# A retention layer and its feed-forward network on one core: the second batch also in halves of 64 tokens, and keys and values loaded head by head for a whole batch

## The chip, the core and the metric

The kernel runs on one core of one Trainium2 chip. The metric is the device time of one execution in microseconds (us), the median over runs. The core has a matrix engine (PE, with its weight loads PEld), a vector engine (DVE), a scalar engine (ACT), GpSimd (POOL), and a sync engine (SP) which here does nothing but issue DMAs, in the order in which the program names them. All DMAs of this kernel are issued by SP.

## The reference

Inputs are `q`, `k`, `v` of shape 4 batches x 8 heads x 768 tokens x 64, and the weights `w_in` (512 x 2048) and `w_out` (2048 x 512). All are float32.

```python
gamma = 1.0 - 2.0 ** (-5.0 - np.arange(H, dtype=np.float32))
for t in range(S):
    state = gamma[None, :, None, None] * state + np.einsum('bhd,bhe->bhde', k[:, :, t], v[:, :, t])
    y[:, :, t] = scale * np.einsum('bhd,bhde->bhe', q[:, :, t], state)
...
h = np.maximum(x @ w_in, 0.0)
return (h * h @ w_out).astype(np.float32)
```

`x` is `y` with the heads side by side: 3072 tokens x 512.

## The kernel before, in words

**Chunks.** Each batch is cut into 6 chunks of 128 tokens, 24 chunks in all, numbered `m` = 0 to 23. The recurrence becomes matrix products within a chunk (scores of `q` against `k`, masked, times `v`) plus the product of `q` with the state that the chunks before have left. Powers of gamma are multiplied into `q` and `k` beforehand by DVE. A matrix product needs `q` and `k` with the head dimension on the partitions, so both are transposed.

**Three ways to attend.** Chunks 0 to 3 go in pairs before the main loop (the `_pair` functions). Chunks 4 to 11 (`attend`, line 941) keep the 128 tokens of a chunk whole: two heads share the partitions in a block diagonal of keys (`k_bd`), the scores are two groups of 4 products of 128 columns, the state is 4, the outputs are 12 (8 in the first chunk of a batch, which has no state yet). In chunks 4 to 7 PE transposes `q` and `k` (`transpose_q` line 362, `transpose_k` line 376) and ACT copies the result; in chunks 8 to 11 a DMA transposes (`dma_transpose_q` line 390, `dma_transpose_k` line 398) and DVE spreads `k` over the diagonal (`spread_k` line 404). Chunks 12 to 23 (`attend2`, line 953) cut a chunk into two halves of 64 tokens and put a pair of heads on the 128 partitions: the scaled keys lie in block-diagonal tiles `ks_bd2s` (`scale_k2` line 638), the values are cast by POOL in three operations (`cast_v2` line 653), the keys are transposed by one DMA of the whole block diagonal (`transpose_k2` line 662, tile `kT`), the scores are one group of 8 products of 64 columns (`scores2` line 671), the state is 4 products for each half (`state2` line 698), the outputs are 16 of 64 columns (`outputs2` line 720).

**Feed-forward network.** It works on blocks: one of 4 chunks, then ten of 2. `ffn_pieces` (line 806) yields after every piece: 4 to 16 products with `w_in` (line 777) with a ReLU on ACT (line 786) and a square on DVE (line 757), or 4 products with `w_out` (line 835). Block 0 has 28 pieces in the loop, every later block 16: eight of the first product, eight of the second.

**The order of work** is written out by hand. `put(place, ...)` (line 930) hangs a step on a place; `before(n)` (line 1000) issues the steps of place `n` after piece `n` and ahead of piece `n+1`. Pieces 5 to 32 are block 0, 33 to 48 block 1, 49 to 64 block 2, 65 to 80 block 3, 81 to 96 block 4, and so on. Every engine, and SP's queue of DMAs, runs its own instructions strictly in this order.

**Transfers.** A load of `q` (`load_q`, line 89) brings 2 chunks, 512 KB. Chunks 4 to 11 load `k` and `v` by chunk, one DMA of 256 KB each (`load_kv`, line 107). Chunks 12 to 23 load them by groups of 3 chunks, 16 DMAs of 96 KB a group, one for a head (`group_loads`, line 121), in tiles `kg` and `vg` of their own. The eight quarters of the weights pass as float32 through a pool of 5 buffers of 1 MB (`wstage`, lines 141 to 153) and are cast to bf16 by DVE, ACT and POOL; a quarter's load waits until the buffer's earlier quarter has been cast. `pack_constants` (line 237) computes the tables that `attend2` needs, at place 50.

Of the kernel before, what the change touches and what calls it, by code (L numbers as in the profile page):

```python
# [9 lines left out]
FP32 = mybir.dt.float32  # L10
BF16 = mybir.dt.bfloat16
# [3 lines left out]
ALU = mybir.AluOpType  # L15
# [4 lines left out]
LDBUFS = 4  # L20

# [3 lines left out]
DMA_FROM = 8  # L25


PACK_FROM = 12

GROUP = 3  # L30
# [3 lines left out]
def kernel(  # L34
# [9 lines left out]
    nc = tc.nc  # L44
    P = nc.NUM_PARTITIONS

    B, H, S, D = q.shape
    DM, DFF = moe_w_in.shape
    C = 128
    NCH = S // C  # L50
    NPAIR = H // 2
    NFB = DFF // 128
    NCB = DM // 128
    NQ = 4
    FPQ = NFB // NQ
    FQ = DFF // NQ
    chunks = [(b, i) for b in range(B) for i in range(NCH)]
    NCHUNK = len(chunks)
# [3 lines left out]
    scale = 1.0 / float(np.sqrt(D))  # L62
# [4 lines left out]
    ldpool = ctx.enter_context(tc.tile_pool(name="ldpool", bufs=LDBUFS // 2))  # L67
    grpool = ctx.enter_context(tc.tile_pool(name="grpool", bufs=2))
    qspool = ctx.enter_context(tc.tile_pool(name="qspool", bufs=2))
    kspool = ctx.enter_context(tc.tile_pool(name="kspool", bufs=4))  # L70
# [6 lines left out]
    wstage = ctx.enter_context(tc.tile_pool(name="wstage", bufs=5))  # L77
# [9 lines left out]
    raw_q, raw_k, raw_v = {}, {}, {}  # L87
# [33 lines left out]
    def group_loads(m):  # L121

        b, i = chunks[m]
        for name, src, to in (("kg", k, raw_k), ("vg", v, raw_v)):
            t = grpool.tile([P, 2 * GROUP, NPAIR, D], FP32, name=name)
            for h in range(H):
                p, hh = divmod(h, 2)
                rows = slice(64 * hh, 64 * (hh + 1))
                nc.sync.dma_start(
                    t[rows, :, p, :],  # L130
                    src[b, h, i * C : (i + GROUP) * C, :].rearrange("(w s) d -> s w d", s=64),
                )
                yield
            for j in range(GROUP):
                to[m + j] = t[:, 2 * j : 2 * j + 2].rearrange("s u p d -> s (u p) d")

    w_in_v = moe_w_in.rearrange("(cb p) f -> p cb f", p=P)
# [3 lines left out]
    def load_w_in(g, parts=1):  # L141
        t = wstage.tile([P, NCB, FQ], FP32, name="w_stage")
        n = FQ // parts
        for j in range(parts):
            nc.sync.dma_start(
                t[:, :, j * n : (j + 1) * n], w_in_v[:, :, g * FQ + j * n : g * FQ + (j + 1) * n]
            )
        staged["in", g] = t

    def load_w_out(g):  # L150
        t = wstage.tile([P, FPQ, DM], FP32, name="w_stage")
        nc.sync.dma_start(t[:], w_out_v[:, g * FPQ : (g + 1) * FPQ, :])
        staged["out", g] = t
# [16 lines left out]
    halves = [slice(0, 64), slice(64, 128)]  # L170
# [160 lines left out]
    def scale_q(m):  # L331
        b, i = chunks[m]
        qs = qspool.tile([P, 2, H, D], BF16, name="qs")
        nc.vector.tensor_tensor(  # L334
            out=qs[:],
            in0=raw_q.pop(m).rearrange("s h r d -> s r h d"),
            in1=qf[:, i : i + 2, :, None].to_broadcast([P, 2, H, D]),
            op=ALU.mult,
        )
        at[m]["qs"] = qs  # L340

    def scale_kv(m):
        b, i = chunks[m]
        ks = kspool.tile([P, H, D], BF16, name="ks")
        nc.vector.tensor_tensor(
            out=ks[:],
            in0=raw_k.pop(m)[:],
            in1=kf[:, i, :, None].to_broadcast([P, H, D]),
            op=ALU.mult,
        )  # L350
        v_bd = v_bds[m % 2]
        vn = raw_v.pop(m)
        nc.gpsimd.tensor_copy(  # L353
            v_bd[:, :, ::3, :], vn.rearrange("s (p hh) d -> s p hh d", hh=2)
        )
        at[m].update(ks=ks, v_bd=v_bd)
# [40 lines left out]

    def dma_transpose_k(m):
        a = at[m]
        kT = kTpool.tile([P, 2 * NPAIR, C], BF16, name="kT")  # L400
        nc.sync.dma_start_transpose(kT[:, 0:NPAIR], a["ks"].rearrange("s h d -> s (h d)"))
        a["kT"] = kT

    def spread_k(m):
        a = at[m]
        kT = a.pop("kT")
        k_bd = k_bds[m % 2]
        for hh in range(2):
            rows = slice(64 * hh, 64 * (hh + 1))
            nc.vector.tensor_copy(k_bd[rows, :, hh, :], kT[rows, 0:NPAIR])  # L410
        a["k_bd"] = k_bd
# [91 lines left out]
    def scale_pair_q(m, r, engine=nc.vector):  # L503
        b, i = chunks[m]
        if r == 0:
            at[m]["qs"] = qspool.tile([P, 2, H, D], BF16, name="qs")
        engine.tensor_tensor(
            out=at[m]["qs"][:, r],
            in0=raw_q[m].rearrange("s h r d -> s r h d")[:, r],
            in1=qf[:, i + r, :, None].to_broadcast([P, H, D]),  # L510
            op=ALU.mult,
        )

    def scale_pair_k(m, r):
        b, i = chunks[m]
        at[m]["ks"] = pair_view(ks_bd2s[m // 2])
        nc.vector.tensor_tensor(
            out=at[m]["ks"][:, r],
            in0=raw_k[m][:, r],
            in1=kfp[:, i + r, :, None].to_broadcast([P, H, D]),  # L520
            op=ALU.mult,
        )
# [115 lines left out]
    def scale_k2(m):  # L638
        b, i = chunks[m]
        ks = ks_bd2s[m % 2]  # L640
        kn = raw_k.pop(m)
        for hh, rows in enumerate(halves):
            nc.vector.tensor_tensor(  # L643
                out=ks[rows, :, hh, :],
                in0=kn[rows],
                in1=kf2[rows, i].rearrange("s u p -> s (u p)")[:, :, None].to_broadcast(
                    [64, 2 * NPAIR, D]
                ),
                op=ALU.mult,
            )  # L650
        at[m]["ks"] = ks

    def cast_v2(m):
        vn = raw_v.pop(m)
        v2 = v2pool.tile([P, 2 * NPAIR, D], BF16, name="v2")
        nc.gpsimd.tensor_copy(v2[:], vn[:])  # L656
        v_bd = v_bd2s[m % 2]
        for hh, rows in enumerate(halves):
            nc.gpsimd.tensor_copy(v_bd[rows, :, hh, :], vn[rows])  # L659
        at[m].update(v2=v2, v_bd=v_bd)  # L660
# [210 lines left out]
    scale_pair_q(0, 0)  # L871
    scale_pair_q(0, 1)
# [8 lines left out]
    scale_pair_q(2, 0, nc.gpsimd)  # L881
    scale_pair_q(2, 1, nc.gpsimd)
# [47 lines left out]
    def put(place, what, *args):  # L930
        parts.setdefault(place, []).append((what, args))

    def attend_q(m, scaled, transposed):
        if m % 2 == 0:
            put(scaled, scale_q, m)
            put(transposed, dma_transpose_q if m >= DMA_FROM else transpose_q, m)

# [3 lines left out]
    def attend(m, scaled, places):  # L941
        by_dma = m >= DMA_FROM
        attend_q(m, scaled, scaled if by_dma else places[0])
        put(places[0], scale_kv, m)
        if by_dma:
            put(places[0], dma_transpose_k, m)
        put(places[1], spread_k if by_dma else transpose_k, m)
        put(places[2], scores, m, 0)
        put(places[3], scores, m, 1)
        put(places[3], state, m)  # L950
        put(places[4], outputs, m)

    def attend2(m, d):
        attend_q(m, d - 17, d - 15)
        put(d - 15, scale_k2, m)
        put(d - 15, cast_v2, m)
        put(d - 13, transpose_k2, m)
        put(d - 6, state2, m, 0)
        put(d - 5, scores2, m)
        put(d - 3, state2, m, 1)  # L960
        put(d, outputs2, m)
# [3 lines left out]
    for m, place in ((5, 10), (6, 14), (7, 18)):  # L965
        put(place, load, m)
# [7 lines left out]
    attend(6, 30, (33, 35, 37, 39, 42))  # L974
    attend(7, None, (40, 42, 44, 46, 49))
    put(50, pack_constants)
    for j, t in enumerate([s_bds[2]] + ks_bd2s + v_bd2s):
        for hh in range(2):
            put(51 + 3 * j + hh, zero_off_diagonal, t, hh)


    done = [55, 62, 70] + [78 + 8 * j for j in range(13)]
    for m, place in ((8, 29), (9, 31), (10, 36)):
        put(place, load, m)
    for m, d in zip(range(8, NCHUNK), done):
        if m < PACK_FROM:
            attend(m, d - 15 if d < 70 else d - 16, (d - 13, d - 7, d - 5, d - 3, d))
        else:
            attend2(m, d)
        if m + 3 < PACK_FROM:  # L990
            put(d - 13, load, m + 3)
        elif m + 3 < NCHUNK and (m + 3) % 2 == 0:
            put(d - 13, load_q, m + 3)
    for m, place in zip(range(PACK_FROM, NCHUNK, GROUP), (43, 67, 92, 116)):
        loads = group_loads(m)
        for j in range(2 * H):
            put(place + 3 * j // 2, next, loads)
        put(place + 3 * H, next, loads, None)
# [43 lines left out]
```

## Time and profile before

| what | us |
|---|---|
| median of 3 runs | 215.21 (214.72 to 242.04) |
| the profiled execution's own time | 214.73 |
| its span | 212.9 |
| PE busy in the span | 204.5 |
| ACT busy | 116.2 |
| DVE busy | 129.4 |
| POOL busy | 50.6 |

The 1.8 us between span and time lie before the first and after the last instruction. The profile gives, for each engine, when an instruction started, how long it ran, and what ended the idle time ahead of it. For SP it gives when a DMA was issued, how long the issue took, and when the data had landed. A "granted clock" of 1.00 means that PE ran at full speed, 0.50 at half. A row with "x4" holds four equal instructions. PE's matrix products overlap in time, so the cost of a group is read from the start of one group to the start of the next, which is what the chain of waits prints.

### The profile page before, as it was taken

To read this page: it belongs to the slowest core of one execution; us is meant where nothing else is said; L and a number is where in the kernel's file an instruction comes from. 1 tells how busy PE (TensorE), PEld (TensorE's weight loads), DVE (VectorE), ACT (ScalarE), POOL (GpSimd) and SP (SyncE) were. 2 spreads that over 40 slices of the span, in tenths; PEclk is the share of its full clock that TensorE was granted. 3 is DMA by queue.
4 is the path that set the end of the run, shared out by engine and by line. 5 is a ranking of instruction groups with operands and counts; after the bars stand their busy time and mean duration, and the time that the engine had idled before them with its cause. 6 is when DMAs were issued, how large, how long until landed. Compare 5 with 4: busy or idle time off the path is not lost.

```text
span 212.9 us, 5128 instructions
## 1 busy us (share of the span) xinstructions
PE 204.5 (96%) x2077; PEld 142.1 (67%) x2077; DVE 129.4 (61%) x257; ACT 116.2 (55%) x216; POOL 50.6 (24%) x106
## 2 busy tenths in 40 slices
PE   5789999999999999999999999999999999999994
PEld 1467644558966975875875875875965965965853
DVE  4777875265585696796495595593694693640410
ACT  8365885358853643652663663652753754643631
POOL 5332466221110411025121323008122223000000
PEclk9889999999999999999999999999999999999999
DMA  6999999999969898599698698998795452401102
GB/s 162 290 317 383 386 386 258 293 242 274 276 172 201 199 197 145 161 207 182 164 197 191 154 189 188 152 194 202 164 240 127 99 80 72 102 0 49 52 0 99
DMA packets 90551, 39.65 MB, mean 186 GB/s; under 512 B 66336, under 2 KB 84000, under 8 KB 90528
## 3 DMA queue, kind: packets, MB, share of 16 engines
q1 hardware_dynamic: 90528, 39.33, 79.4%
q8 instruction: 16, 0.26, 0.6%
q14 instruction: 7, 0.06, 0.1%
HBM read 27.26 MB, written 6.29 MB: 158 GB/s over the span
## 4 chain that ended last, share of the span: by engine, by line
PE 90%; ACT 2%; DVE 2%; DMA 2%; POOL 1%; issue 1%; POOLq 0%; ACTq 0%; DVEq 0%
PE psf L835 38%; PE psf L777 38%; DMA qn<-in_q_dram 2%; PE st L421 2%; PE y L484 1%; PE st L681 1%; PE y L737 1%; PE y L730 1%; PE c_ps L708 1%; PE y L313 1%; DVE pt L568 1%; PE c_ps L585 1%; PE psf L544 1%; ACT osb L845 1%; PE c_ps L447 1%
## 5 line engine op out<-in xcount | busy, mean ns | idle before, releaser
L777 PE MATMUL psf<-xt,w_in_bf 128*128 128x256 bf16 (+2 forms) x880 | 90.7, 259 | 0.2 <-ACT xt L492 0.2
L835 PE MATMUL psf<-w_out_bf,h 128*128 128x512 bf16 (+2 forms) x400 | 89.6, 371 | 0.0
L777 PEld LDWEIGHTS <-w_in_bf 128*128 128x128 bf16 x880 | 71.3, 98 | 11.8 <-issue 0.3
L786 ACT ACTIVATE h<-psf 128x512 bf16<-128x512 f32 x96 | 57.0, 597 | 22.2 <-PE psf L777 19.6
L835 PEld LDWEIGHTS <-h 128*128 128x128 bf16 x400 | 36.3, 98 | 35.1
L757 DVE TENSOR_TENSOR h<-h 128x512 bf16<-128x512 bf16 x96 | 43.1, 467 | 21.0 <-ACT h L786 20.2
L845 ACT ACTIVATE osb<-psf 128x512 f32<-128x512 f32 (+2 forms) x25 | 14.5, 580 | 28.6 <-PE psf L835 28.6
L718 DVE CAST s_bd<-c_ps 64x256 bf16<-64x256 f32 x22 | 9.4, 427 | 27.4 <-ACT s_bd L717 27.1
L656 POOL CAST v<-vg 128x512 bf16<-128x512 f32 x12 | 8.1, 674 | 56.3 <-PE c_ps L708 21.0
L659 POOL CAST v_bd<-vg 64x512 bf16<-64x512 f32 x24 | 16.4, 682 | 15.0 <-PE y L737 14.1
L428 DVE TENSOR_TENSOR pt<-st,cmask 128x512 bf16<-128x512 f32 x16 | 11.1, 692 | 12.5 <-PE st L421 12.3
L643 DVE TENSOR_TENSOR ks_bdp<-kg,kf 64x512 bf16<-64x512 f32 x24 | 18.3, 762 | 0.4
L353 POOL CAST v_bd<-vn 128x512 bf16<-128x512 f32 x8 | 5.7, 718 | 36.2 <-PE y L484 29.1
L744 ACT ACTIVATE xt<-y 128x512 bf16<-128x512 f32 x12 | 8.9, 742 | 9.6 <-PE y L737 9.6
L334 DVE TENSOR_TENSOR qs<-qn,qf 128x1024 bf16<-128x1024 f32 x10 | 12.1, 1213 | 2.1 <-DMA qn<-in_q_dram 2.0
L717 ACT ACTIVATE s_bd<-c_ps 64x256 bf16<-64x256 f32 x22 | 8.1, 367 | 8.8 <-PE c_ps L708 8.8
L301 POOL CAST w_out_bf<-w_stage 128x512 bf16<-128x512 f32 x12 | 7.8, 689 | 5.5 <-DMA w_stage<-in_moe_w_out_dram 5.5
L492 ACT ACTIVATE xt<-y 128x512 bf16<-128x512 f32 x8 | 6.0, 749 | 5.5 <-PE y L484 5.2
L688 DVE TENSOR_TENSOR pt<-st,cmask 128x512 bf16<-128x512 f32 x12 | 8.3, 691 | 0.4
L313 PE MATMUL y<-ident 128*128 128x512 bf16 (+1 forms) x13 | 5.8, 558 | 2.1 <-POOL ident L199 2.1
L708 PEld LDWEIGHTS <-ks_bdp 128*128 128x128 bf16 x88 | 5.6, 98 | 2.6
L737 PE MATMUL y<-pt,v_bd 128*128 128x64 bf16 x96 | 7.0, 193 | 0.0
(99 smaller groups left out, 167.1 us busy)
## 6 DMA issues: line engine op xcount, KB each, us to landing
qn<-in_q_dram SPq DMA_DIRECT2D x12, 512.0 KB, 4.9
out_dram<-osb SPq DMA_DIRECT2D x23, 256.0 KB, 2.5
w_stage<-in_moe_w_out_dram SPq DMA_DIRECT2D x4, 1024.0 KB, 12.2
w_stage<-in_moe_w_in_dram SPq DMA_DIRECT2D x3, 1024.0 KB, 11.8
kg<-in_k_dram SPq DMA_DIRECT2D x32, 96.0 KB, 3.6
vg<-in_v_dram SPq DMA_DIRECT2D x32, 96.0 KB, 3.4
kn<-in_k_dram SPq DMA_DIRECT2D x8, 256.0 KB, 5.6
vn<-in_v_dram SPq DMA_DIRECT2D x8, 256.0 KB, 5.6
```

Source lines behind the costliest of these rows:

```text
L334: nc.vector.tensor_tensor(out=qs[:], in0=raw_q.pop(m).rearrange("s h r d -> s r h d"), in1=qf[:, i : i + 2, :, None].to_broadcast([P, 2, H ...
L428: nc.vector.tensor_tensor(out=a["pt"][:, 2 * half : 2 * half + 2], in0=st[:], in1=cmask.rearrange("s r t -> s (r t)")[:, None, None, :].to ...
L643: nc.vector.tensor_tensor(out=ks[rows, :, hh, :], in0=kn[rows], in1=kf2[rows, i].rearrange("s u p -> s (u p)")[:, :, None].to_broadcast([6 ...
L659: nc.gpsimd.tensor_copy(v_bd[rows, :, hh, :], vn[rows])
L718: nc.vector.tensor_copy(s_bd[halves[1], :, 1, :], c[halves[1]])
L737: nc.tensor.matmul(yv, lhsT=a["v_bd"][:, u * NPAIR + p], rhs=a["pt"][:, u * NPAIR + p, :].rearrange("s (r t) -> s r t", r=2), start=not inter,
L744: nc.scalar.activation(xts[tb][:, :, off : off + C].rearrange("e p (s r) -> e p r s", r=2), y[:], AF.Copy,)
L757: nc.vector.tensor_mul(hv, hv, hv)
L777: nc.tensor.matmul(hp, lhsT=w_in_bf[g][:, cb, fq * 128 : (fq + 1) * 128], rhs=xts[tb][:, cb, cols], start=(cb == 0), stop=(cb == NCB - 1),)
L786: nc.scalar.activation(hv, hp[:], AF.Relu)
L835: nc.tensor.matmul(op[:], lhsT=h_of(tb, f)[:, 0, j * C : (j + 1) * C], rhs=w_out_bf[g][:, fq, cols], start=(f == 0), stop=(f == NFB - 1),)
L845: nc.scalar.activation(osb[:, cols], op[:], AF.Copy)
```

## The change

- Chunks 6 to 11 go the way of `attend2` as well (`PACK_FROM` is 6 instead of 12). `dma_transpose_k` and `spread_k` are gone; the DMA transposes of `q` begin with chunk 6 instead of 8, those of `k` too, and those of `k` in chunks 8 to 11 are of the full block diagonal.
- `k` and `v` of a batch are loaded by `batch_loads`: 8 DMAs for `k`, 8 for `v`, one for a head, 192 KB each. For the second batch they are split in two sets: first the part of chunks 6 and 7 (16 DMAs of 64 KB), later that of chunks 8 to 11 (16 of 128 KB).
- These tiles come from the pool of the weights' quarters, now called `stage`, which has 4 buffers instead of 5. The pools of the groups are gone.
- `q` is scaled in two instructions of half the size, at two places.
- `pack_constants` moves from place 50 to place 14, the clearing of the diagonals from places 51 to 64 to places 15 to 24.
- The outputs of chunks 6 to 11 move: places 42, 49, 55, 62, 70, 78 become 47, 52, 57, 62, 70, 78.

```diff
-PACK_FROM = 12
-GROUP = 3
+PACK_FROM = 6
...
-    wstage = ctx.enter_context(tc.tile_pool(name="wstage", bufs=5))
+    stage = ctx.enter_context(tc.tile_pool(name="stage", bufs=4))
...
+    def batch_loads(m, name, ends):
+        b, i = chunks[m]
+        src, to = (k, raw_k) if name == "k" else (v, raw_v)
+        t = stage_tile(2 * NCH * NPAIR * D)
+        t = t.rearrange("s (p w d) -> s p w d", p=NPAIR, d=D)
+        for j in range(NCH):
+            to[m + j] = t[:, :, 2 * j : 2 * j + 2].rearrange("s p u d -> s u p d")
+        for w0, w1 in zip([0] + ends, ends):
+            for hh, rows in enumerate(halves):
+                for p in range(NPAIR):
+                    nc.sync.dma_start(
+                        t[rows, p, 2 * w0 : 2 * w1],
+                        src[b, 2 * p + hh, w0 * C : w1 * C].rearrange("(w s) d -> s w d", s=64),
+                    )
+                    yield
...
-    def attend2(m, d):
-        attend_q(m, d - 17, d - 15)
-        put(d - 15, scale_k2, m)
-        put(d - 15, cast_v2, m)
-        put(d - 13, transpose_k2, m)
-        put(d - 6, state2, m, 0)
+    def attend2(m, d, before, q_at, k_at, turn_at, v_at):
+        if m % 2 == 0:
+            put(q_at, scale_q, m, 0)
+            put(q_at + 1, scale_q, m, 1)
+            put(q_at + 2, dma_transpose_q, m)
+        put(k_at, scale_k2, m)
+        put(v_at, cast_v2, m)
+        put(turn_at, transpose_k2, m)
+        put(max(d - 6, before), state2, m, 0)
         put(d - 5, scores2, m)
         put(d - 3, state2, m, 1)
         put(d, outputs2, m)
...
-    attend(6, 30, (33, 35, 37, 39, 42))
-    attend(7, None, (40, 42, 44, 46, 49))
-    put(50, pack_constants)
+    put(14, pack_constants)
...
+    put(12, load_q, 6)
+    put(30, load_q, 8)
+    put(41, load_q, 10)
+    done = [47, 52, 57, 62] + [70 + 8 * j for j in range(14)]
+    ahead = {6: (34, 35, 39), 7: (37, 38, 44), 8: (47, 48, 48), 9: (52, 53, 53), 10: (57, 59, 58)}
+    for m, d in zip(range(PACK_FROM, NCHUNK), done):
+        attend2(m, d, done[m - PACK_FROM - 1] if m > PACK_FROM else 0,
+                d - 17 if m < 8 else d - 18, *ahead.get(m, (d - 15, d - 13, d - 15)))
+        if m >= 12 and m % 2 == 0:
+            put(d - 29, load_q, m)
+    places = {
+        (6, "k"): [13 + j // 3 for j in range(8)] + [39 + j // 2 for j in range(8)],
+        (6, "v"): [16 + j // 3 for j in range(8)] + [43 + j // 2 for j in range(8)],
+        (12, "k"): [52 + j for j in range(8)],
+        (12, "v"): [60 + j for j in range(8)],
+        (18, "k"): [84 + 2 * j for j in range(8)],
+        (18, "v"): [100 + 2 * j for j in range(8)],
+    }
```

The numbers that `ahead` gives for a chunk are the places of the scaling of its keys, of the DMA that transposes them, and of the cast of its values. In SP's queue the change leaves, between the load of `q` of chunk 6 and the transpose of chunk 8's keys, this order: 16 loads of 64 KB, 2 stores, `q` of chunk 8, 2 stores, the transposes of `q` 6, `k` 6 and `k` 7, 4 loads of 128 KB, `q` of chunk 10, the transpose of `q` 8, 6 loads of 128 KB, a store, 6 loads of 128 KB, a store.

## The prediction

> **What bounds the kernel now.** I read the page first, then the stretches between the blocks, the chain of waits in order of time, and SP's queue. The page says that PE is the bound:
>
> ```profile
> PE 204.5 (96%) x2077; PEld 142.1 (67%) x2077; DVE 129.4 (61%) x257; ACT 116.2 (55%) x216; POOL 50.6 (24%) x106
> ```
>
> The stretches (columns: length, then busy time and count of PE, PEld, DVE, ACT, POOL, granted clock, DMA share, GB/s) show where it can be shortened:
>
> ```profile
> 5.20:8.60 3.40, 1.85 (x18) 1.01 (x18) 2.46 (x4) 1.77 (x4) 0.00 (x0) 1.00 1.22 290
> 8.70:12.00 3.30, 3.30 (x42) 2.00 (x43) 2.93 (x6) 1.15 (x2) 2.04 (x2) 0.50 1.22 290
> ...
> 67.70:85.56 17.86, 17.59 (x223) 13.62 (x220) 12.83 (x33) 9.02 (x16) 3.91 (x16) 1.00 0.92 191
> 85.56:102.04 16.48, 16.48 (x147) 11.95 (x145) 12.18 (x21) 7.80 (x14) 4.27 (x6) 1.00 0.98 177
> 102.04:117.69 15.65, 15.65 (x159) 11.15 (x157) 10.76 (x19) 8.51 (x17) 3.20 (x6) 1.00 0.94 184
> ```
>
> From 102.04 on chunks 12 to 23 are attended in halves and PE has no gap; nothing there can change but by a wait. The DMA engines are almost always busy up to there (share 0.92 to 0.98), so transfers have little room. The first two rows come back below.
>
> The chain gives PE's price of each step, from the start of one group to the next:
>
> ```profile
> 39.45 0.45 PE tp L367 x8
> 41.62 0.22 PE tp L380 x4
> 43.57 0.22 PE st L421 x4
> 45.74 0.22 PE c_ps L447 x4
> 61.13 0.45 PE y L484 x8
> 67.70 0.89 PE psf L777 x16
> 72.43 0.38 PE st L421 x4
> 102.92 0.23 PE st L681 x8
> ```
>
> Twelve products of outputs cost 0.67 (53.21 to 53.88 in the timeline of PE), sixteen narrow ones 0.47 (123.11 to 123.58), twelve narrow ones 0.35 in proportion, the narrow state 0.11 (120.38 to 120.49).
>
> SP's queue (start, length, issue):
>
> ```profile
> 41.42 0.96 SPq L113 DMA_DIRECT2D kn<-in_k_dram  x1
> 42.42 1.16 SPq L113 DMA_DIRECT2D vn<-in_v_dram  x1
> ...
> 60.56 0.37 SPq L113 DMA_DIRECT2D kn<-in_k_dram  x1
> ...
> 68.54 1.96 SPq L129 DMA_DIRECT2D kg<-in_k_dram  x3
> 70.60 0.56 SPq L847 DMA_DIRECT2D out_dram<-osb  x1
> 71.26 2.48 SPq L401 DMA_TRANSPOSE kT<-ks  x1
> 73.79 0.57 SPq L94 DMA_DIRECT2D qn<-in_q_dram  x1
> ```
>
> An issue costs SP about the same whatever it moves: 0.65 for 96 KB of one head, 0.57 for 512 KB. And the queue already runs behind: the transpose at 71.26 had its keys scaled at 68.3.
>
> **PE's work.** Whole chunks cost: chunk 6 half of 0.45, 0.22, 2 x 0.22, 0.22, 0.45 = 1.56; chunk 7 the same with 0.67 for outputs = 1.78; 8 to 10 without PE's transposes 1.33 each; 11, which gives no state on, 1.11. Together 8.44. In halves: chunk 6 0.23 + 2 x 0.11 + 0.35 = 0.80; 7 to 10 0.92 each; 11 0.81; together 5.29. Saved on the path: **3.15**. The wait at 72.43 (0.27) also goes: DVE was late there because it waited for POOL's tables, which now come at place 14. **-0.27.**
>
> **Tables and clearing at places 14 to 24.** They cost POOL about 2 us between the casts of two quarters of `w_out`; the second then ends near 35.8 instead of 33.8, and its first use is the fifth piece of the second product, near 36.9. ReLUs wait for the exponential about 1 us, and four buffers of PE's results cover that. 0; at most 1.
>
> **Four weight buffers.** The first quarter of `w_out` is issued at 19.2 (when a buffer is cast) instead of 14.29. In the queue of transfers it lands behind the last of `w_in` (26.45) at 29.15 either way, and is needed cast at 33.4. 0; at most 3.5, if the 4.9 of delay came through but for the slack of 1.4.
>
> **DVE, ACT, POOL.** Scaling keys in halves (2 x 0.69 for 0.68), casting values (3 x 0.61 for 0.69), splitting `q` (2 x 0.70 for 1.22) lie beside PE: DVE is busy 12.8 of 17.9 us, POOL 3.9. 0. The later loads (places 52 to 114) are fewer than the groups' and as large. 0.
>
> **SP's queue between places 13 and 48.** Here I expect the loss. From 41.42 (start of chunk 6's `k`, which the same transfers precede as before): 16 loads at 0.65 = 10.4, 4 stores at 0.61, `q` of chunk 8 at 0.63 gives 54.9. The transposes follow: `q` 6 at 1.6, to 56.5, and `k` 6 at 1.35, issued at 56.5. Landings:
>
> ```profile
> L665 SPq DMA_TRANSPOSE kT<-ks_bdp x12: 1239/1292/2412, 95.2 to 181.5; - x12
> ...
> DMA to landing us min/median/max: 3.1/3.4/4.6
> ```
>
> So `k` 6 lands at 59.9. PE wants it at place 42, which was at 61.13 and comes 1.33 - 0.11 earlier, 59.9. **0**, bounds 0 and 1.2. Then `k` 7 to 59.2, and, ahead of `k` 8, 16 loads (10.4), `q` 10 (0.63), the transpose of `q` 8 (1.6), 2 stores (1.2): `k` 8 is issued at 73.0 and lands at 76.4. PE comes to these scores (place 52) at: 67.70, less 2.66 and plus 1.14 of chunks 6 and 7 in block 1, four pieces at 0.89, and 0.11 + 0.47 + 0.11: 70.4. **PE waits 6.0.** Behind the scores in PE's queue stands all of block 2, so nothing fills this. On DVE the scaling of chunk 8's keys waits for their last load (about 69), with squares of block 2 behind it; the second product wants those from place 56 on, which PE's own wait covers. The same place needs the cast values of chunk 8, whose last load is issued near 72: the same lateness by another way.
>
> Bounds: with the shortest landing and slightly shorter issues 4.7; with the longest landing 7.2. Far below: if such a load cost only the 0.37 + 0.05 of the row at 60.56, SP would be held only by the scaled keys of chunk 7 (57.0), `k` 8 would land at 71.9, wait 1.5. I take 6.0, since the one-head loads (0.65) are the nearest row. Transfers alone would not rescue it: at 1.2 between landings of 256 KB loads, the same list from 60.4 ends near 75.
>
> **After the wait.** `k` 9 is scaled behind chunk 8's mask on DVE: 0.4 + 0.69 + 1.4 + 0.1 + 3.4 = 6.0 against 5.35 of PE's work up to its scores: 0.65. `k` 10 comes in time (10.8 against 11.3 after `k` 9's issue), bounds 0 and 1.9. The clock adds more: in 5.20 to 8.60 PE stood idle 1.55 of 3.40 us, and ran the next 3.4 at clock 0.50. A wait of 6 us should bring one such stretch, worth up to 1.7, partly spent while PE still waits, and hiding the 0.65. For clock and `k` 9 together I take **1.2**, bounds 0.3 and 2.4.
>
> The Trainium skill ("TensorE: Matmul & The Clock Gate", Part 1) has the clock at half after one idle window of about 3.4 us, and the window running free of the kernel. By that rule a stretch 46% idle would not have slowed PE, as the row above shows it did; read strictly, a whole window falls into a wait of 6.0 in (6.0 - 3.4)/3.4 = 76 of 100 cases, and in the others the sum holds 0.65 in place of 1.2 and ends at 217.9.
>
> **Sum.** -3.15 - 0.27 + 0 + 6.0 + 1.2 = +3.8. The profiled execution took 214.73 (span 212.9 and 1.8 around it), 0.5 under the median of 215.21: **218.5**.
>
> **Rivals.**
> - *The queue keeps up* (other side). Issue at 0.42 a load: a wait of 1.5 or less at place 52, no cold clock: 214.73 - 3.42 + 1.5 = 212.8. Without any wait PE would still stand 0.7 at place 52, as outputs, copy (0.74, behind a ReLU of 0.60) and first product follow close: 212.0. It decides against me if `k` 8 is issued by 70.4. For: loads are contiguous in the buffer now, the 256 KB row shows 0.37 after a pause. Against: back to back that kind takes 0.57 too. Chance 0.18.
> - *Loss and gain cancel*: a wait of 3 to 4 with a warm clock, 214 to 216. Chance 0.17.
> - *It snowballs*: longest landings (7.2), `k` 10 late by 1.9, cold clock 1.7: +7.4, 222.1. For: the DMA share is 0.98 already. Chance 0.10.
> - *The start is hurt*: late `w_out` or tables, +3 on top: 221.5. Against: the slack above. Chance 0.05.
>
> **Chances.** My forecast (216.2 to 220.5) has 0.50. About 2% is what a measurement of this kernel can tell from no change: 210.9 to 219.5 against the median. The gain's ceiling is 3.4, so faster by over 2% is hardly in reach: 0.03. Slower by over 2% has the two last rivals and the upper part of the forecast, 0.15 + 0.18 = 0.33. The rest, 0.64, is within 2%. The range 212.0 to 221.5 leaves out most of the snowball.
>
> **What would show it.** Right: PE idle several us ahead of the first scores of chunk 8 on a transposed `kT` or the cast values; SP without pause from 41 to 73; a stretch at clock 0.50 near 77; blocks from 102 on as long as before. Wrong: one-head loads issued at 0.4; `k` 8 issued before 70; idle PE in block 0; or a PE saving other than 3.15.

## The result, and the profile after

The changed kernel takes 232.87 us (median of 4 runs, 231.88 to 233.93), the kernel before 214.97 beside it: a ratio of 1.084, 95% interval 1.077 to 1.091. It is slower, and outside the forecast range of 212.0 to 221.5. One of the four runs of the kernel before took 242.04 us; ratio and interval leave it out. The profiled execution took 233.93. The page of it begins:

```profile
span 232.1 us, 5193 instructions
...
PE 207.5 (89%) x2087; PEld 143.2 (62%) x2109; DVE 133.3 (57%) x265; ACT 114.6 (49%) x217; POOL 59.2 (25%) x118
...
PE 66%; DMA 15%; SPq 9%; POOL 3%; issue 2%; DVE 2%; ACT 1%; POOLq 0%; ACTq 0%; DVEq 0%
```

The last line is the share of each engine in the chain that ended last: transfers (DMA) and SP's issuing (SPq) now hold 24% of it (8 of these belong to the load of `w_out` at the start, through a wait of 0.64 us). Before, PE held 90% and DMA 2%. The span grew by 19.2 us; PE's busy time by 3.0 of these, its idle time by the rest. Where, the stretches of both kernels show (columns as in the prediction), first the kernel after:

```profile
43.00:55.00 12.00, 11.16 (x136) 8.29 (x134) 7.72 (x13) 7.53 (x14) 2.75 (x4) 1.00 0.57 133
55.00:84.50 29.50, 17.84 (x221) 12.56 (x220) 11.24 (x21) 9.29 (x18) 6.03 (x9) 0.84 1.11 213
84.50:109.00 24.50, 20.40 (x200) 15.10 (x203) 13.28 (x24) 8.25 (x16) 6.80 (x10) 0.78 1.01 152
109.00:160.00 51.00, 50.68 (x516) 37.09 (x520) 34.46 (x67) 27.95 (x52) 11.42 (x18) 1.00 1.13 197
```

The kernel before in the same stretches:

```profile
43.00:55.00 12.00, 11.81 (x148) 9.10 (x147) 6.80 (x11) 8.57 (x16) 2.45 (x4) 1.00 1.23 270
55.00:84.50 29.50, 29.23 (x351) 21.91 (x349) 20.82 (x46) 15.64 (x29) 4.66 (x17) 1.00 0.89 190
```

After 109 PE is as full as ever. Before that, two things stand out. From 43 to 55, where SP issues 64 KB loads one by one, the DMA engines move 133 GB/s, half of what they moved before; from 55 on they are busy most of the time, with a gap that is shown below, and PE waits. PE's timeline has these waits (in brackets: idle us and what ended it):

```profile
63.47 0.41 PE L646 MATMUL st<-qT,kT 128*128 128x64 bf16 x8 [3.13 <-DMA kT<-ks_bdp]
...
83.57 0.37 PE L673 MATMUL c_ps<-v,ks_bdp 128*128 128x64 bf16 x4 [7.87 <-POOL v L619]
84.51 0.61 PE L646 MATMUL st<-qT,kT 128*128 128x64 bf16 x8 [0.57 <-DMA kT<-ks_bdp]
...
103.80 0.61 PE L646 MATMUL st<-qT,kT 128*128 128x64 bf16 x8 [3.98 <-DMA kT<-ks_bdp]
```

They stand ahead of chunks 6, 8 (cast values, then keys) and 10: 15.6 us together. SP's queue says why they are late (start, how long the issuing took, what was issued):

```profile
59.23 3.53 SPq L630 DMA_TRANSPOSE kT<-ks_bdp  x2
...
75.46 3.57 SPq L132 DMA_DIRECT2D stage<-in_v_dram  x4
79.13 0.65 SPq L812 DMA_DIRECT2D out_dram<-osb  x1
79.89 1.75 SPq L630 DMA_TRANSPOSE kT<-ks_bdp  x1
81.73 0.61 SPq L132 DMA_DIRECT2D stage<-in_k_dram  x1
87.61 1.25 SPq L630 DMA_TRANSPOSE kT<-ks_bdp  x1
...
93.78 3.74 SPq L132 DMA_DIRECT2D stage<-in_k_dram  x2
...
97.63 4.02 SPq L630 DMA_TRANSPOSE kT<-ks_bdp  x1
```

Chunk 6's keys are transposed at 59.23 (forecast 56.5), the last values of chunks 8 to 11 are issued at 78.4, chunk 8's keys at 79.89 (forecast 73.0). Then SP stands from 82.4 to 87.6 for chunk 9's scaled keys, with the loads of chunk 12 behind it. DVE shows why these keys are late: it takes the mask of chunk 8 first, and that waits for PE's scores.

```profile
85.16 0.69 DVE L653 TENSOR_TENSOR pt<-st,cmask 128x512 bf16<-128x512 f32 x1 [0.34 <-PE st L646]
85.77 1.78 DVE L608 TENSOR_TENSOR ks_bdp<-stage,kf 64x512 bf16<-64x512 f32 x2
```

Meanwhile the transfers run dry. In this window (columns as above) the DMA engines move nothing at all:

```profile
85.18:88.60 3.42, 3.42 (x37) 3.42 (x35) 3.36 (x6) 0.63 (x2) 1.76 (x3) 0.50 0.00 0
```

The loads behind then go out in a bunch and fill the queue (two issues take 3.74, the transpose 4.02), which makes chunk 10's keys late. Each wait hands the next one on.

### The profile page after: what moved, and what is told of

It is laid out like the page before. It is cut to its first block, busy times and chain, and to the rows that moved or that the text cites. A ratio compares the mean times of both kernels' runs of the same rounds, so it can differ in the third digit from the quotient of the medians.

```text
span 232.1 us, 5193 instructions
## 1 busy us (share of the span) xinstructions
PE 207.5 (89%) x2087; PEld 143.2 (62%) x2109; DVE 133.3 (57%) x265; ACT 114.6 (49%) x217; POOL 59.2 (25%) x118
## 4 chain that ended last, share of the span: by engine, by line
PE 66%; DMA 15%; SPq 9%; POOL 3%; issue 2%; DVE 2%; ACT 1%; POOLq 0%; ACTq 0%; DVEq 0%
PE psf L742 30%; PE psf L800 27%; DMA stage<-in_moe_w_out_dram 8%; SPq L132 5%; DMA kT<-ks_bdp 5%; POOL w_out_bf L302 2%; DMA kn<-in_k_dram 2%; PE st L646 2%; PE y L702 2%; PE y L695 2%; SPq L630 2%; PE c_ps L673 1%; SPq L389 1%; DVE pt L533 1%; PE psf L509 1%
## 5 line engine op out<-in xcount | busy, mean ns | idle before, releaser
L619 POOL CAST v<-stage 128x512 bf16<-128x512 f32 x18 | 12.3, 683 | 91.0 <-DMA stage<-in_v_dram 60.8
L622 POOL CAST v_bd<-stage 64x512 bf16<-64x512 f32 x36 | 24.3, 676 | 26.2 <-PE y L702 25.2
L608 DVE TENSOR_TENSOR ks_bdp<-stage,kf 64x512 bf16<-64x512 f32 x36 | 27.1, 753 | 2.9 <-DMA stage<-in_k_dram 2.4
L333 DVE TENSOR_TENSOR qs<-qn,qf 128x512 bf16<-128x512 f32 x22 | 15.5, 714 | 2.6 <-DMA qn<-in_q_dram 2.4
L673 PE MATMUL c_ps<-v,ks_bdp 128*128 128x64 bf16 x132 | 9.7, 199 | 7.9 <-POOL v L619 7.9
L653 DVE TENSOR_TENSOR pt<-st,cmask 128x512 bf16<-128x512 f32 x18 | 12.5, 692 | 6.0 <-PE st L646 5.6
L646 PE MATMUL st<-qT,kT 128*128 128x64 bf16 x144 | 7.6, 198 | 7.7 <-DMA kT<-ks_bdp 7.7
L646 PEld LDWEIGHTS <-kT 128*128 128x128 bf16 x144 | 6.6, 101 | 10.4 <-DMA kT<-ks_bdp 8.6
L702 PE MATMUL y<-pt,v_bd 128*128 128x64 bf16 x144 | 10.6, 193 | 0.0
L695 PE MATMUL y<-qT,s_bd 128*128 128x64 bf16 x132 | 10.1, 193 | 0.0
L302 POOL CAST w_out_bf<-stage 128x512 bf16<-128x512 f32 x12 | 8.6, 758 | 5.5 <-DMA stage<-in_moe_w_out_dram 5.5
```

Of the source, the lines that this page charges most:

```text
L333: engine.tensor_tensor(out=out, in0=by, in1=table[:, :, None].to_broadcast([P, H, D]), op=ALU.mult)
L608: nc.vector.tensor_tensor(out=ks[rows, :, hh, :].rearrange("s (u p) d -> s u p d", u=2), in0=kn[rows], in1=kf2[rows, i, :, :, None].to_bro ...
L622: nc.gpsimd.tensor_copy(v_bd[rows, :, hh, :].rearrange("s (u p) d -> s u p d", u=2), vn[rows])
L646: nc.tensor.matmul(st[:, c, :], lhsT=kT[:, c, :], rhs=half_of(a["qT"], p, u), start=True, stop=True,)
L673: nc.tensor.matmul(c[:, p, :], lhsT=a["ks"][:, u * NPAIR + p], rhs=a["v2"][:, u * NPAIR + p, :], start=(i == 0 and u == 0 and p == 0), sto ...
L695: nc.tensor.matmul(yv, lhsT=s_bds[(2 * m + u - 1) % 3][:, p], rhs=half_of(a["qT"], p, u), start=True, stop=False,)
```

## The experiments

My theory on seeing this was a shortage of transfer time from 45 to 115 us. Rivals: the number of issues, the size of the pieces, the clock, the order of the queue. All times are single runs unless an interval is given; the kernel before took 214.4 to 215.2 beside them. The diffs are shortened to what matters, with remarks behind a #. Some versions give a chunk its tokens in another order, or others than its own, as their expectations say; they measure time and do not compute the layer.

**Pieces of 1 to 2 KB instead of 256 bytes** (as many loads):

```diff
-    src[...].rearrange("(w s) d -> s w d", s=64)
+    src[...].rearrange("(s w) d -> s w d", s=64)      # second batch only
```

> The loads of the second batch's k and v are as many as before and in the same places, but each partition takes neighbouring tokens, so that a piece is 1 to 2 KB instead of 256 B (the tokens within a set are permuted, so the output is another one). If SP's issue of about 0.65 us a load and its strict order set the lateness, the issue of chunk 8's transpose stays near 79 and the time at 229 to 233 us. If the transfers of small pieces set it, the waits at chunks 6, 8 and 10 fall from 3.1, 8.4 and 4.0 us to about 1, 3 and 2, and the time to about 222.

232.79 us, with waits of 3.3, 7.1 + 1.1 and 4.8. With the loads as they are, the size of the pieces is not what makes the second batch late.

**One load for four heads** (8 loads instead of 32, of 256 and 512 KB):

```diff
-    for p in range(NPAIR): nc.sync.dma_start(t[rows, p, ...], src[b, 2 * p + hh, ...])
+    nc.sync.dma_start(t[rows, :, ...], src[b, hh::2, ...].rearrange("p (s w) d -> s p (w d)", s=64))
```

> As the run with long pieces (the tokens within a set are permuted), and also one DMA for four heads: 8 loads instead of 32 for the second batch, the same bytes. If the number of issues sets the lateness, 24 x 0.65 = 15.6 us of SP's queue go, the transposes of chunks 6 to 11 are in time, and the time is 211.5 to 214, which is also the test of the 3.15 us of PE's work saved. If the transfers set it, the same as the run with long pieces.

228.34 us. Chunk 6's wait is gone; chunk 8 still waits 8.0 + 0.6 for values, chunk 10 3.9. The loads of 512 KB landed 2.2 to 3.0 us apart. The number of issues, or what goes with it, explains chunk 6, not the rest.

**Idle products to hold the clock up**, first ahead of the scores of chunks 6, 8, 10:

> The changed kernel with idle products of 512 columns ahead of the scores of chunks 6, 8 and 10 (14, 36 and 18 of them, as long as the waits), nothing else changed. If half the clock costs what the trace shows (20.5 us at 0.50, in which PE worked about 12.8 us, so 6.4 lost), the granted clock stays at 1.00 and the time falls to 226 to 229, less than 6.4 since a faster PE waits longer for a queue that is no faster. If the slow stretches lie in the shadow of the waits, it stays at 231 to 233.

242.75 us, a run that answers nothing on the clock: the filler of chunk 8 stood behind the wait it should fill (the state comes first) and added 10.6 us, from 83.50 to 94.09. SP then stood 14.4 us for chunk 9's keys. With the filler ahead of chunk 8's state:

```diff
+    filler = {42: (scores2, 14), 52: (state2, 36), 65: (scores2, 18)}
+    if n in filler and what is filler[n][0]:
+        keep_awake(filler[n][1], pool=ps_f, name="psf")
```

> As the run with idle products, but those of chunk 8 stand ahead of its state, which is what waits first (on the cast values), not of its scores. They now run while PE would wait anyway. If half the clock was a cost of its own, the clock stays at 1.00, the waits end at the same times, and the time is 226 to 229 us. If the transfers alone set when PE goes on, a faster PE only waits longer: 231 to 233.

232.59 us at full clock, with 0.3 to 0.9 us of idle time left ahead of the three fillers' chunks, so that no filler held PE up: in this kernel the three stretches of half clock cost nothing. The whole of it in one stretch:

```profile
55.00:109.00 54.00, 50.83 (x534) 33.53 (x532) 29.30 (x51) 20.01 (x39) 13.33 (x18) 1.00 1.09 187
```

PE is full and at full clock, the transfers are as late as before. A slow PE between waits for transfers only shortens the next wait.

**The second batch in one set** (16 loads of 192 KB early):

> k and v of the second batch in one set of 16 loads of 192 KB at places 13 to 18, instead of 16 of 64 KB and 16 of 128 KB later: the same bytes, 16 issues fewer between chunk 7's transpose and chunk 8's. If SP's issues set the lateness, the wait at chunk 8 goes (8.4 us and the slow clock behind it), that at chunk 6 grows by some 4 us since 192 KB land slower than they are issued, and the time is 222 to 227. If the transfers set it, the bytes ahead of chunk 8's transpose are the same and so is its landing near 84: 230 or more.

235.76 us. Chunk 6 now waits 8.8 + 2.9, chunk 8 only 3.0, chunk 10 4.8: the bytes ahead of a chunk move the wait, they don't remove it.

**Without the 16 loads of chunks 8 to 11:**

> The 16 loads of 128 KB of chunks 8 to 11 are left out, and those chunks read the k and v of chunks 6 and 7 instead (another output). If these loads, 2 MB in front of chunk 8's transpose in SP's queue, set the waits at chunks 8 and 10 (7.9 + 0.6 and 4.0 us, with the slow clock behind them), both go, chunk 6 keeps its 3.1 and one stretch at half the clock (1.7): 214.97 - 3.4 + 4.8 = 216, and PE's blocks show the 3.15 saved. If the wait at chunk 8 is of other make (scaling of keys, cast, transposes), it stays above 4 us and the time above 220.

224.63 us, between the two expectations. So this set is worth 8 us. What is left, ahead of chunks 6, 8 and 10:

```profile
62.38 0.41 PE L647 MATMUL st<-qT,kT 128*128 128x64 bf16 x8 [2.77 <-DMA kT<-ks_bdp]
...
76.04 0.41 PE L647 MATMUL st<-qT,kT 128*128 128x64 bf16 x8 [2.98 <-DMA kT<-ks_bdp]
...
95.08 0.41 PE L647 MATMUL st<-qT,kT 128*128 128x64 bf16 x8 [4.92 <-DMA kT<-ks_bdp]
```

Chunk 10's wait is of its own: its transpose stood behind the loads of chunk 12, and its issue alone took 4.0 us.

**Both halves of a head pair in one load:**

> The loads of the second batch with both halves of the partitions in one DMA: 16 instead of 32, long pieces, all 128 partitions (tokens within a set are permuted, so the output is another one). Beside the merged run (8 loads, long pieces, 64 partitions, 512 KB each landing in 2.2 to 3.0 us) it tells whether filling 64 partitions alone is what makes these transfers slow. If it is, 256 KB land in about 0.8 us, chunk 8 waits under 2 us and the time is 213 to 218. If not, 1.1 to 1.5 us each and 226 to 230.

274.58 us, for a reason of its own (last section); it says nothing on partitions.

**Another division of the sets and places** (sets of chunks 6 to 8 and 9 to 11, keys scaled earlier, stores issued by ACT):

> The changed kernel with its transfers in another order and the same bytes: sets of chunks 6 to 8 and 9 to 11 (96 KB a load), q of chunk 8 behind the transpose of k 6, k of the second set between the transposes of k 7 and k 8, its v behind k 8, transposes of k 8 to 10 a few places earlier, stores issued by ACT. If the bytes that stand ahead of each transpose set the waits, that at chunk 6 goes (3 us less ahead of it), that at chunk 8 falls to 0 to 2 us, chunk 9 waits 0 to 2 instead, the clock stays at 1.00, and the time is 211.5 to 216. If SP or the transfers are short of time altogether, the waits move to chunks 9 and 10 and the time stays above 222.

231.05 us. The waits spread; the two largest, 2.55 and 3.26 us, now stand ahead of chunks 11 and 12, later than any in the changed kernel.

Up to here the theory of a plain shortage held. The next runs took the change apart.

**Loads chunk by chunk, in the order of use** (24 of 128 KB, the same buffers):

```diff
+    for m, k_at, v_at in ((6, 13, 14), (7, 15, 16), (8, 33, 34), (9, 39, 41), (10, 44, 46), (11, 49, 51)):
+        ...    # two loads of k at k_at, two of v at v_at, each of 4 heads x 128 tokens
```

> Chunks 6 to 11 are loaded chunk by chunk in the order in which they are used (two loads of 128 KB for k, two for v, 24 in all instead of 32 of 128 and 256 KB), into the same buffers; the tokens of a chunk come in another order, so the output is not the reference's. If the transfers as a whole are too slow for this stretch (my theory so far), the same bytes and transposes still have to pass: the waits get smaller but stay, 222 us or more. If it is that a set is needed whole (the first chunk of a set waits for loads that belong to later ones), the waits ahead of chunks 6 and 8 fall below 0.5 us each and 4 us at chunk 10 is all that is left: 214 to 219.

222.87 us, at the edge of the first expectation: chunk 6's wait is gone, 3.5 at chunk 8 and 3.2 at chunk 10 remain. Bytes and transposes are those of the changed kernel, so 10 of its 18 us are not a plain shortage. Three things changed together: the order, the number of loads, and the pieces, now of 512 bytes. Longer pieces alone gave nothing (232.79), fewer loads 4.5 with longer pieces (the run with 8); so the order of use probably gives the larger part. No run changed the order alone.

**Chunk 12's loads later:**

> Only the loads of 192 KB of chunks 12 to 17 and the q of chunk 12 move: from places 52 to 67 to places 61 to 70. If the wait ahead of chunk 10 comes from their standing ahead of its transpose in SP's queue, it falls from 4.0 us to under 1, and the time to about 229. If the transfers are short as a whole, it falls too but comes back as 2 to 4 us ahead of chunk 12 (near 118 us), and the time stays at 231 to 234.

237.02 us, worse than both expectations, though chunk 10's wait is gone as foreseen. SP's queue:

```profile
78.59 8.93 SPq L630 DMA_TRANSPOSE kT<-ks_bdp  x2
87.91 1.23 SPq L389 DMA_TRANSPOSE qT<-qs  x1
94.87 1.23 SPq L630 DMA_TRANSPOSE kT<-ks_bdp  x1
```

With nothing ahead of them to issue, SP stands 6.0 and 5.6 us for scaled keys (inside the first row, and ahead of 94.87) with the loads of chunk 12 behind these transposes; they then collide with chunk 11's keys (a wait of 5.5 us at 112.4), and chunk 12 waits 3.1. Chunk 8's wait is 10.0 here. Transfer time is lost standing, not only used up.

**The load scheme of chunks 12 to 23 alone, on the kernel before:**

```diff
-    group_loads(m)                             # 3 chunks, 96 KB a load, 16 loads over 24 places
+    batch_loads(12, ...), batch_loads(18, ...)  # 6 chunks, 192 KB a load, 16 loads over 16 places from 52, four buffers
```

> The kernel before with one part of the change: chunks 12 to 23 loaded head by head for a whole batch at the places of the changed kernel, into four buffers shared with the weights; chunks 4 to 11 as before. If this part is innocent: 213 to 217 us, no wait over 0.6 us. If the loads of 192 KB on 64 partitions are by themselves too slow, a wait of 3 to 5 us near 100 us and 218 us or more.

219.82 us: 5.4 us for a part that I had priced at nothing. Its wait ahead of chunk 11, the products behind it, and the queue ahead of it:

```profile
97.73 0.69 PE L427 MATMUL st<-qT,k_bd 128*128 128x128 bf16 x4 [2.48 <-DVE k_bd L416]
98.23 3.58 PE L841 MATMUL psf<-w_out_bf,h 128*128 128x512 bf16 x8
```

```profile
82.31 3.14 SPq L136 DMA_DIRECT2D stage<-in_k_dram  x3
85.54 0.59 SPq L853 DMA_DIRECT2D out_dram<-osb  x1
86.18 3.90 SPq L136 DMA_DIRECT2D stage<-in_v_dram  x4
...
92.13 1.56 SPq L407 DMA_TRANSPOSE kT<-ks  x1
```

The loads of 192 KB that went out from 86.18 on land 1.1 to 1.3 us apart (at 91.52, 92.77, 94.06 and 95.15), which is more than the 0.65 of an issue, so the queue fills and SP is held (3.90 for four). Chunk 11's keys were scaled at 88.5, their transpose goes out at 92.13. The wait is 2.5 of the 5.4 us. Behind it PE is granted half the clock from 98.2 to 101.6 (the eight products take 3.58, eight take 1.89 elsewhere); it is busy all that time, so about 1.7 us more are lost, and here no later wait takes them up. The run changes size, places and buffers together: it prices the scheme, not the size of a load.

**Chunks 6 to 11 transposed by TensorE:**

> The changed kernel, but the keys of chunks 6 to 11 are transposed by TensorE (eight products a chunk and two copies on ScalarE), not by a transfer: six block-diagonal transposes leave the queue, and SP no longer stands for scaled keys there. TensorE gets about 6 x 0.5 = 3 us more to do. If these transposes and SP's standing for their keys make the lateness, the waits (3.1, 8.4 and 4.0 us) fall to 8 us together or less and the time to 227 us or less. If it is the loads' own transfer time, the wait for chunk 8's values stays at 6 us or more and the time is 231 us or more.

231.16 us. Chunk 10's wait is gone; chunk 8 waits 2.2 for its scaled keys and still 4.3 for its values. Neither expectation holds cleanly: the wait for the values shrank below 6 us, the time hardly moved, as PE has more to do and waits for ACT's copies (0.7 to 0.95, six times). Taking six transposes off the queue is no cure.

The last six runs change the version loaded chunk by chunk. **Keys of chunks 8 to 10 scaled and transposed earlier:**

```diff
-    8: (47, 48, 48), 9: (52, 53, 53), 10: (57, 59, 58)
+    8: (45, 46, 48), 9: (50, 51, 53), 10: (55, 56, 58)
```

> As the kernel loaded chunk by chunk (222.87 us, one wait of 3.5 us ahead of chunk 8, one of 3.2 ahead of chunk 10; tokens of a chunk in another order, so the output is not the reference's), with one more edit: the keys of chunks 8, 9 and 10 are scaled and transposed two to four places earlier. If its wait ahead of chunk 8 is the distance of five places between scaling and scores (keys were there at 64.0, SP issued the transpose at 69.1), it falls below 1 us, and only chunk 10's is left: 218.5 to 220.5. If the transfers as a whole are short, the wait comes back elsewhere: 222 or more.

224.13 us (ratio 1.044, interval 1.041 to 1.047), as the second expectation has it: no better than without. Chunk 8's wait is gone (0.4 left) and so is chunk 10's, but chunk 11's keys now go out behind the 192 KB loads, and PE waits 7.2 us there:

```profile
102.53 0.61 PE L664 MATMUL st<-qT,kT 128*128 128x64 bf16 x8 [7.17 <-DMA kT<-ks_bdp]
```

**Chunks 12 to 23 in groups of three, as before the change:**

> As the kernel loaded chunk by chunk (222.87 us), with one more edit: chunks 12 to 23 are loaded in groups of three by 96 KB, as in the kernel before, instead of six by 192 KB. If the loads of chunk 12's batch cost what they cost alone (5 us), the wait of 3.2 us ahead of chunk 10 goes and the time is 217 to 219. If the second batch's own loads and transposes make the lateness, the wait stays at 2 us or more and the time at 221 or more.

219.40 us: 3.5 less, chunk 10 no longer waits, chunk 8 does (4.8). **Both edits:**

> Both edits of the two runs beside it: what is left of the change is the arithmetic by halves, six block-diagonal transposes and four weight buffers. If those are innocent, no wait over 0.6 us, TensorE's saving of 3.4 us comes through: 210.5 to 213. If the transposes and the loads on 64 partitions alone are too much, waits of 3 us or more together remain: 215 or more.

218.09 us (ratio 1.016, interval 1.010 to 1.022), the second expectation. One large wait is left, ahead of chunk 8, and SP's queue before it points to the order:

```profile
74.40 0.61 PE L680 MATMUL st<-qT,kT 128*128 128x64 bf16 x8 [3.79 <-DMA kT<-ks_bdp]
```

```profile
64.17 1.28 SPq L150 DMA_DIRECT2D stage<-in_v_dram  x2
65.55 0.60 SPq L164 DMA_DIRECT2D stage<-in_k_dram  x1
66.24 0.56 SPq L846 DMA_DIRECT2D out_dram<-osb  x1
66.86 1.26 SPq L150 DMA_DIRECT2D stage<-in_k_dram  x2
68.16 0.62 SPq L164 DMA_DIRECT2D stage<-in_k_dram  x1
68.89 1.27 SPq L664 DMA_TRANSPOSE kT<-ks_bdp  x1
```

Chunk 8's keys were scaled at 64.9; the six loads and a store between 64.17 and 68.89 are for later chunks.

**The same with tokens in their order, 48 loads of 64 KB:**

> As the run before it in this list, with the tokens in their order, for which each load of 128 KB becomes two of 64 KB (48 loads instead of 24 for chunks 6 to 11), output as the reference's. If the number of issues is free as long as SP stands for nothing, 211 to 214. If SP's 0.65 us an issue decides, 24 x 0.65 = 16 us more of its queue between places 13 and 51 bring waits of 4 to 9 us back: 216 to 222.

233.19 us (ratio 1.085, interval 1.081 to 1.090), beyond both expectations. All that had been won is lost again: chunk 6's keys are issued at 63.90, behind eight loads of chunk 8 at 0.65, and PE waits 7.3 there. On SP's one queue the order of use was worth something only with few issues.

**Order mended.** Keys of chunks 8 to 10 are transposed right after their scaling, `q` of chunk 8 three places earlier (not five, as the expectation says), `q` of chunk 10 is scaled two places later, and the loads are spread anew:

```diff
-    (8, 33, 34), (9, 39, 41), (10, 44, 46), (11, 49, 51)    # q of chunk 10 loaded at 41
+    (8, 30, 32), (9, 38, 40), (10, 46, 48), (11, 51, 53)    # q of chunk 10 loaded at 46
```

> As the run with both edits (218.09 us, one wait of 3.8 us ahead of chunk 8, whose keys were scaled at 64.9 while SP reached their transpose only at 68.9), with the order on SP mended: q of chunk 8 transposed five places earlier, keys of chunk 8 transposed right after their scaling, the loads of chunk 10 two places later (tokens of a chunk still in another order). If only the order made that wait, it goes, and what remains of the change is the saving of 3.4 us: 210.5 to 213.5, faster than the kernel before. If the halves bring a shortage of transfer time by themselves, 2 us or more of waiting appear elsewhere: 215 or more.

216.66 us (ratio 1.0086, interval 1.0058 to 1.0114). Chunk 8's wait is gone, so the order made it. But time and waits are those of the second expectation: of the large waits nothing is left, and small ones stand elsewhere, ahead of chunks 6, 9 and 11:

```profile
61.25 0.41 PE L680 MATMUL st<-qT,kT 128*128 128x64 bf16 x8 [1.15 <-DMA kT<-ks_bdp]
...
78.96 0.41 PE L680 MATMUL st<-qT,kT 128*128 128x64 bf16 x8 [1.00 <-DMA kT<-ks_bdp]
...
97.17 0.41 PE L680 MATMUL st<-qT,kT 128*128 128x64 bf16 x8 [1.30 <-DMA kT<-ks_bdp]
```

The page has the saving of the halves, at full clock all through:

```profile
PE 201.9 (94%) x2087; PEld 139.2 (65%) x2109; DVE 133.5 (62%) x265; ACT 114.4 (53%) x217; POOL 61.5 (29%) x118
```

2.6 us of PE's work are saved, and 4.8 us of small waits from 41 us on (0.45 before) take them back. So some shortage of transfers through the halves themselves is not excluded. The kernel before stays the fastest of all.

**The same order with the tokens right, values issued by GpSimd's queue:**

> The same order with the tokens in their order: 48 loads of 64 KB instead of 24 of 128 KB, those of v issued by GpSimd's queue, so that SP issues no more than in the run beside it. If SP's issues are what made the version with 48 loads slow (233.2 us), 211 to 216. If loads of 64 KB in pieces of 256 bytes are too slow in the transfers themselves, or GpSimd's issuing holds up the casts of v and of the weights, 219 or more, with a wait of 3 us or more ahead of chunk 6 or 8.

222.94 us (ratio 1.036, interval 1.032 to 1.040), the second expectation but for the chunks: waits of 2.6 and 3.1 are left ahead of chunks 6 and 9. It takes 10 us less than the other run with 48 loads. Three things differ between them: SP issues only half of the loads, the values of chunks 6 and 7 are loaded at later places, and the order is the mended one, which was worth 1.4 with 24 loads (218.09 to 216.66). So SP's issuing is probably most of that loss. What makes the 6 us to 216.66, the shorter pieces, the smaller loads or GpSimd's issuing, was not tried.

In sum, by runs: 232.87; loaded in order of use with 24 loads 222.87; chunks 12 to 23 in groups again 219.40; scaled earlier 218.09; SP's order mended 216.66; before 215. So about 16 of the 18 us are in how the loads were cut and ordered, and the rest is small waits, most of them for keys. How those divide between the six block-diagonal transposes and the shorter distances was not settled. The steps from 222.87 to 216.66 all have the tokens of a chunk in another order; with the tokens right the best run took 222.94, 10 us less than the change and 8 more than the kernel before. That the other 6 can be had with the right output is not shown.

## Why the prediction was wrong, point by point

The mechanism was named, with its place: "PE idle several us ahead of the first scores of chunk 8 on a transposed `kT` or the cast values", a stretch at half clock near 77, blocks as long as before later on. All three came. The size failed, by 14 us, and two of the three waits were priced at nothing. Added up, the profiled span grew by 19.2 us where 3.8 were forecast: waits of 3.1, 8.4 and 4.0 ahead of chunks 6, 8 and 10, 0.6 for `w_out`, 3.0 more of busy PE, less the 0.3 for the tables, which is all but 0.3.

- **PE's work, -3.15**: about right. The mended order shows 2.6. In the changed kernel PE's busy time grew by 3.0, but 13.2 us of it were at half clock, which at full clock would be 6.6 less, so by this estimate it would have fallen by 3.6.
- **Wait for the tables, -0.27**: gone, as said. **Tables at place 14, four weight buffers, 0**: nearly. A product with the last quarter of `w_out` waited 0.64 at 45.3 in the changed kernel and not in the mended one, within the bound of 3.5.
- **"The later loads (places 52 to 114) are fewer than the groups' and as large. 0."**: wrong. This is the step that failed most plainly: on the kernel before, alone, it costs 5.4 us, and taking it back gave 3.5 (222.87 to 219.40). I counted issues and bytes. But 192 KB took 1.1 to 1.3 us to pass and 0.65 to issue, so the queue fills and whatever stands behind, here a transpose with PE waiting for it, goes out late.
- **SP's queue between places 13 and 48**, chunk 6's keys, 0 (at most 1.2): 3.1. The first load went out at 42.9 and not 41.4, sixteen loads took 0.70 each and not 0.65, the transpose of `q` 6 2.15 and not 1.6: 2.7 us of lateness in the issue of chunk 6's keys. Their own issue took 2.18 and not 1.35, and PE had them 4.2 after its start and not 3.4. Each number came from a row that I had read as a price, and the same issues took longer here. The row of 2.48 for a transpose stood in the prediction itself.
- **The wait at chunk 8, 6.0 (4.7 to 7.2)**: 7.9 + 0.6. The keys went out 6.9 later than forecast, but PE, held up by chunk 6 and at half clock behind it, also came 5.3 later. Of the two causes I had named, the cast values ended it first.
- **After the wait, 1.2 (0.3 to 2.4)**: chunk 10 waited 4.0 where I had at most 1.9. I let SP go on issuing during PE's wait. It can't: it stands for scaled keys, DVE scales them in the order of the places, and PE's wait holds up the places. So a wait delays the loads for the next one. The rival "it snowballs" (0.10, 222.1) had the same chain of late chunks; it was right in kind and too small, because it was bounded with landing times and not with SP's standing, 9.1 us in five waits of SP:

```profile
SPq L630 <- DVE ks_bdp L608: 9.1, 5, 5.2
```

- **The clock, up to 1.7**: half clock came in three stretches. In the changed kernel it cost nothing, as the run at full clock shows; with the load scheme alone, where no later wait took it up, it cost about the 1.7 of the forecast. The windows that matter (busy PE first after the length):

```profile
61.30:64.71 3.41, 1.24 (x13) 0.74 (x14) 2.36 (x5) 0.00 (x0) 0.00 (x0) 1.00 1.07 221
64.71:68.12 3.41, 3.41 (x14) 1.33 (x12) 0.43 (x1) 0.86 (x2) 0.00 (x0) 0.50 0.67 147
...
74.95:78.36 3.41, 0.76 (x22) 0.73 (x20) 2.21 (x5) 1.25 (x3) 0.00 (x0) 1.00 1.25 221
78.36:81.77 3.41, 0.00 (x0) 0.00 (x0) 0.00 (x0) 0.00 (x0) 0.00 (x0) 0.50 1.31 187
...
98.84:102.25 3.41, 0.98 (x12) 0.63 (x8) 0.43 (x1) 1.46 (x3) 0.00 (x0) 1.00 1.47 109
```

The window ahead of each drop was idle 64, 78 and 71%, never wholly. The Trainium skill ("TensorE: Matmul & The Clock Gate", Part 1) asks for at least one idle window of about 3.4 us; the length agrees with these rows (the drops at 64.71, 78.36 and 102.25 are 4 and 7 times 3.41 apart), but a partly idle window was enough here, as in the row that the prediction set against that rule.

- **"Transfers alone would not rescue it"**: true, and the sentence should have been turned round: with little room for transfers a loss of order costs time, and I used it as a footnote. But the share of 0.92 to 0.98 is no measure of that room: the same column goes above 1 (1.22 at 290 GB/s in the first row of the prediction's stretches, 1.47 at 109 GB/s above), and the changed kernel lost time where it read 0.57 and 0.00.

## What to carry to other kernels

Where one in-order queue issues all transfers, price a load by what stands behind it: ask of every transpose or store which loads are ahead of it, what the issuer itself must wait for, and whether the bytes pass faster than they are issued. Cutting loads by head for several chunks at once makes the first chunk wait for the last one's bytes; load in the order of use, in as few issues as that allows. A saving on the busiest engine, here 3 us, is soon spent where the transfers beside it must be cut and ordered anew for it.

## What the runs showed of the hardware

- Pieces of 256 bytes took longer on the mean beside larger loads. The run with the load scheme alone moves 63,488 of them, as the kernel before does; their mean time in the trace went from 23 to 27 ns (median 18 in both), which over 16 engines is 92.2 and 105.7 us. With 96 KB loads again (mended order) it is 23. Why was not tried.
- Loads whose outer dimension is 2 (both halves of a head pair at once) were slow. The stretch of that run in which SP issued eight of them:

```profile
43.00:66.00 23.00, 15.51 (x199) 12.00 (x197) 10.11 (x18) 10.36 (x18) 2.74 (x4) 0.97 0.27 82
```

82 GB/s at a DMA share of 0.27. The Trainium skill ("DMA: Bandwidth & Descriptors", "Why a DMA increments its semaphore by 16 and not by 1") gives the number of engines as the largest one up to 16 that divides the outermost dimension of both sides, which is 2 here; the run agrees.
- In the last run an issue of a load cost GpSimd's queue what it costs SP's: 2.44 us for four of 64 KB, 0.61 each.
